# Closing a program on GpSimd's wait for the stored result, without the second barrier and without the release of the other engines

## Chip, cores, metric

One core of one Trainium2 chip in each run. The metric is the device time of one execution in microseconds (us), median of several runs; single times to 0.01 us.

## The reference

Decode step of one token, in bfloat16. The sum of three terms is written out as 1024 numbers (2 KB):

```
x   = A_x                                   # 1 x 1 x 1024
xn  = layernorm(x)
out = x + attention(xn, k_cache, v_cache, wq, wo)    # 32 query heads, 4 kv heads, 65536 keys of 128
        + mixer_mlp(xn, w1, w2, w3, w4)
```

The caches and the weights make 169.87 MB of loads, the output 2 KB of store.

## The kernel before: the parts that matter

The body streams weights and caches through three slots of SBUF. Its last act is a cast of the accumulated row and a store from ScalarE's queue:

```
    compute_w4(early, FC)

    out_t = ogpool.tile([64, 512], BF16, name="out_t", tag="og")
    nc.scalar.copy(out=out_t[:], in_=psB[0:64, :])
    nc.scalar.dma_start(out=out[0, 0, :].rearrange("(j n) -> j n", j=2),
                        in_=out_t[:].rearrange("(a b) n -> a b n", b=32)[:, 0, :])
```

Nothing in the kernel's text says how the program ends; the framework appends a closing block of 30 instructions. This is the block as it was built, with the semaphores by number: 109 counts transfers of one lane, the store's among them, 96 is the gather of the barrier, 97 its release. A gather is GpSimd's (Pool's) wait until each of the other four engines has added 1 to 96; the release is its adding of 4 to 97, of which each of the others takes 1 and goes on. The Drains between these steps do no work on data. The clear sets the program's semaphores back.

```
SP          wait 106, 105 | wait 107, 103 | wait 108, 101 | wait 109>=64, 100 | wait 110, 102 | Drain, wait 99
ACT PE DVE SP   Drain, wait 97==0, then 96 += 1        # first gather
ACT PE DVE SP   wait 97>=1, then 97 -= 1               # first release taken
Pool        Drain | wait 96>=4, then 96 -= 4 | 97 += 4 # gather, release
Pool        Drain | range clear of the semaphores
ACT PE DVE SP   Drain, wait 97==0, then 96 += 1        # second gather
ACT PE DVE SP   wait 97>=1, then 97 -= 1
Pool        Drain | wait 96>=4, then 96 -= 4 | 97 += 4
```

Of the kernel before, what the change touches and what calls it, by code (L numbers as in the profile page):

```python
# [59 lines left out]
    entry.instructions = entry.instructions[:at] + [load] + entry.instructions[at:]  # L60


@with_exitstack
def kernel(
    ctx: ExitStack,
# [13 lines left out]
    nc = tc.nc  # L79
    nc.at_finalize(keep_loaded_weights)  # L80
    nc.at_finalize(lead_with_the_first_load)
    D = A_x.shape[-1]
    S = A_x.shape[1]
    HKV = A_k_cache.shape[1]
# [3 lines left out]
    F = B_w3.shape[1]  # L88
    DC = D // P
    FC = F // P  # L90
    UKEYS = P * ROW // DH
    assert DH == P and HQ // HKV == 8 and HKV == 4 and D == 1024 and F == 3584 and S == 1
    assert SK % UKEYS == 0 and sum(W4_PIECES) == FC
# [23 lines left out]
    class Stream:  # L117
# [17 lines left out]
        def load(self, it):  # L135
# [7 lines left out]
            elif it == "w12":  # L143
                go(out=t[:, 0:DC * D], in_=B_w1.rearrange("(p c) n -> p (c n)", c=DC))
                go(out=t[:, DC * D:2 * DC * D], in_=B_w2.rearrange("(m c) n -> m (c n)", c=DC))
            elif it == "wo":
                go(out=t[:].rearrange("p (g n) -> p g n", g=HKV),
                   in_=A_wo.rearrange("(g p j) n -> p g (j n)", g=HKV, p=P))
            elif it == "w4":
                w4_v = B_w4.rearrange("(m c) n -> m c n", c=FC)  # L150
                c0 = 0
                for n in W4_PIECES:
                    go(out=t[:, c0 * D:(c0 + n) * D], in_=w4_v[:, c0:c0 + n, :].rearrange("p c n -> p (c n)"))
                    c0 += n
# [7 lines left out]

    x_row = ogpool.tile([32, D], BF16, name="x_row", tag="og")
    nc.vector.memset(x_row[:], 0.0)
# [322 lines left out]
```

## Time and profile before

| | before |
|---|---|
| time, median of the first 3 runs | 402.19 us (402.04 to 402.21) |
| recorded span, first to last instruction of the program | 400.3 us |
| load queue, share of 16 DMA engines' span | 98.6% |
| closing block after the store has landed | 0.89 us |

Four lines of the profile's page: the span, the two DMA queues (packets, MB, share of 16 engines' span), and what HBM moved; q1 carries the loads, q10 the 2 KB transfers.

```profile
span 400.3 us, 2563 instructions
...
q1 hardware_dynamic: 4560, 169.87, 98.6%
...
q10 hardware_dynamic: 6, 0.00, 0.0%
...
HBM read 169.87 MB, written 0.00 MB: 424 GB/s over the span
```

The kernel is bound by its loads for all but the last 4 us. The chain of waits that ended last, from 380 us on (start, length, what):

```profile
379.33 17.39 DMA big<-in_B_w_dram
396.73 0.04 issue
396.77 0.40 PE psB L191 x2
397.17 0.02 issue
397.19 0.58 ACT out_t L455
```

And the last two instructions that do work, from the timeline (start, length, engine, line, operation):

```profile
397.19 0.58 ACT L455 CAST out_t<-psB 64x512 bf16<-64x512 f32 x1 [29.56 <-PE psB L191]
397.80 0.59 ACTq L456 DMA_DIRECT2D out_dram<-out_t  x1
```

The last load lands at 396.73, the cast starts at 397.19, the store is issued at 397.80. What SyncE's queue waited for from 380 us on (total us, times, longest):

```profile
SPq L482 <- DMA big<-in_B_w_dram: 17.0, 3, 15.8
SPq L482 <- DMA out_dram<-out_t: 2.7, 1, 2.7
SPq L482 <- PEq L482: 0.6, 2, 0.4
```

The second line is the end of the program: SyncE waits for the store. What comes behind it is not busy work, so no group of the page shows it. The trace holds the records all the same. The closing block, read from its instruction and semaphore records (start in us, length, engine):

```
399.439         last increment of 109: the store has landed
399.455 0.028   SP    wait 109            399.938 0.096  Pool  range clear
399.517 0.028   SP    wait 110, 102       400.063 0.034  Pool  Drain
399.582 0.007   SP    Drain, wait 99      400.142 0.017  Pool  gather
399.640 0.007   SP    Drain, 96 += 1      400.220 0.017  Pool  release, ends 400.237
399.672 0.017   Pool  gather              400.262 0.017  SP    release taken
399.751 0.017   Pool  release             400.274 0.051  PE    release taken, ends 400.325
399.832 0.078   Pool  Drain
```

Behind the program the same trace shows updates of semaphore 2, nine at a time, around the resets of all semaphores:

```
first nine updates of 2:   400.588 400.622 400.799 400.843 400.867 400.965 401.003 401.037 401.084
resets                     400.980 to 401.646
second nine updates of 2:  401.870 401.904 401.942 401.987 402.010 402.107 402.146 402.180 402.227
```

The Trainium skill, "Runtime: NRT & Kernel Launch", section "The ~15µs preamble/postamble breakdown", names them: a barrier over the five engines, a reset of the semaphores, another barrier. No record shows where the clock starts or stops.

### The profile page before, as it was taken

The page shows a single profiled execution, that of the slowest core. Times are in us where ns is not written, and L with a number is a line of the kernel's source. Part 1 is how long each engine was busy: PE and PEld are TensorE (multiplying, and loading weights), DVE is VectorE, ACT ScalarE, POOL GpSimd, SP SyncE. Part 2 cuts the span into 40 slices and gives each one's busy share as a digit, 9 for nine tenths or more (in the row PEclk, how much of TensorE's full clock was granted, in tenths as well). Part 3 has the DMA queues.
Part 4 walks back from the last instruction along what each step waited for, and adds up shares of the span by engine and source line. Part 5 has one row for each costly group of instructions (what it writes and reads, how often), then busy time and mean ns, then how long its engine had stood idle before and what let it go on. Part 6 is the DMA issues. An engine that isn't in the chain of part 4 may idle for free.

```text
span 400.3 us, 2563 instructions
## 1 busy us (share of the span) xinstructions
PE 236.0 (59%) x1348; PEld 45.2 (11%) x854; DVE 208.9 (52%) x154; ACT 27.3 (7%) x35; POOL 5.3 (1%) x28
## 2 busy tenths in 40 slices
PE   0561960591678247922965195629453946594986
PEld 0210000010200110011102010201020102000222
DVE  1601010965196549644953994279349931975040
ACT  1001010003000200020002000100100020002000
POOL 2000000000000000000000000000000000000000
PEclk9995795597669666978796789568865986697989
DMA  9998999999999999999999999999999998999895
GB/s 419 419 453 371 435 471 458 426 419 419 421 426 465 452 426 414 426 426 432 445 460 426 419 426 419 447 439 452 426 421 426 432 445 385 432 481 426 385 417 201
DMA packets 4575, 170.01 MB, mean 425 GB/s; under 512 B 467, under 2 KB 469, under 8 KB 982
## 3 DMA queue, kind: packets, MB, share of 16 engines
q1 hardware_dynamic: 4560, 169.87, 98.6%
q8 instruction: 8, 0.13, 0.1%
q14 instruction: 1, 0.01, 0.0%
q10 hardware_dynamic: 6, 0.00, 0.0%
HBM read 169.87 MB, written 0.00 MB: 424 GB/s over the span
## 4 chain that ended last, share of the span: by engine, by line
DMA 51%; DVE 26%; PE 16%; ACT 3%; another core or an unknown queue 2%; issue 1%; DVEq 0%; ACTq 0%
DMA big<-in_A_k_cache_dram 31%; DVE big L327 19%; DMA big<-in_A_v_cache_dram 10%; PE sc L332 8%; PE oacc L382 6%; DMA big<-in_A_wq_dram 6%; DMA big<-in_B_w_dram 4%; DVE p_sb L353 3%; DVE mx L337 3%; ACT p_sb L350 3%; PE psq L257 2%; DVE m L341 0%; PE pm_mx L339 0%; PE pm_mx L346 0%
## 5 line engine op out<-in xcount | busy, mean ns | idle before, releaser
L332 PE MATMUL sc<-big,qdiag 128*128 128x512 bf16 x512 | 129.5, 414 | 62.7 <-DVE big L327 57.2
L327 DVE STREAM_TRANSPOSE big<-big 128x4096 f32<-128x4096 f32 x32 | 139.4, 4413 | 49.4 <-DMA big<-in_A_k_cache_dram 49.4
L382 PE MATMUL oacc<-big,p_sb 128*32 128x512 bf16 x512 | 46.9, 539 | 34.5 <-DVE p_sb L353 34.5
L337 DVE TENSOR_REDUCE mx<-sc 128x1 f32<-128x2048 f32 x8 | 18.3, 2291 | 30.0 <-PE sc L332 30.0
L332 PEld LDWEIGHTS <-qdiag 128*128 128x128 bf16 x128 | 13.2, 103 | 174.7 <-issue 145.9
L350 ACT ACTIVATE p_sb<-sc,nball 128x2048 bf16<-128x2048 f32 x8 | 15.7, 1967 | 217.8 <-DVE nball L348 217.8
L353 DVE STREAM_TRANSPOSE p_sb<-p_sb 128x2048 bf16<-128x2048 bf16 x8 | 18.5, 2311 | 18.0 <-ACT p_sb L350 18.0
L382 PEld LDWEIGHTS <-p_sb 128*32 128x32 bf16 x512 | 17.1, 129 | 61.0 <-DVE p_sb L353 35.1
L257 PE MATMUL psh<-big,ln_rep_b 128*32 128x512 bf16 (+1 forms) x64 | 12.4, 941 | 7.6 <-DMA big<-in_B_w_dram 7.6
L421 PE MATMUL o_acc<-big,oT 128*1 128x512 bf16 x48 | 12.8, 437 | 2.4 <-ACT p_sb L350 2.4
L339 PE MATMUL pm_mx<-ident_f,mx 128*1 128x128 f32 x8 | 2.2, 273 | 19.1 <-DVE mx L337 19.1
L296 DVE STREAM_TRANSPOSE h_row<-h_row 128x896 bf16<-128x896 bf16 x1 | 1.1, 1111 | 20.8 <-ACT h_row L295 20.8
L391 DVE SCALAR_TENSOR_TENSOR og<-oacc,wb,og 128x512 f32<-128x512 f32 x4 | 3.0, 746 | 16.7 <-PE oacc L382 16.7
L191 PE MATMUL psB<-big,hT 128*1 128x512 bf16 x56 | 8.1, 424 | 0.6 <-DMA big<-in_B_w_dram 0.5
L427 DVE COPY o_rows<-o_acc 1x1024 f32<-1x1024 f32 x1 | 1.2, 1211 | 13.6 <-PE oacc L382 13.6
L205 PE MATMUL pm_ln<-ln_rowsum_a,ones_f 128*128 128x1 f32 x2 | 0.6, 348 | 12.5 <-DVE ln_rowsum_a L203 12.5
L403 PE MATMUL pm_e<-ol,sel8big 128*128 128x129 f32 x8 | 2.8, 446 | 7.9 <-DVE ol L402 7.9
L257 PE MATMUL psq<-big,ln_rep_a 128*32 128x512 bf16 x64 | 6.2, 573 | 1.5 <-DMA big<-in_A_wq_dram 1.5
L281 POOL COPY qdiag<-qx 32x32 bf16<-32x32 bf16 x16 | 3.2, 203 | 279.5 <-PE sc L332 249.6
L196 DVE STREAM_TRANSPOSE x_t<-x_row 32x256 bf16<-32x256 bf16 x4 | 2.5, 616 | 8.1 <-DMA x_row<-in_A_x_dram 8.0
L269 DVE CAST q_row<-psq 128x512 bf16<-128x512 f32 x1 | 0.7, 691 | 8.4 <-PE psq L257 8.4
L346 PE MATMUL pm_mx<-ident_f,rep 1*128 1x1 f32 x8 | 1.8, 223 | 5.0 <-DVE rep L343 5.0
(95 smaller groups left out, 73.2 us busy)
## 6 DMA issues: line engine op xcount, KB each, us to landing
big<-in_A_wo_dram SPq DMA_DIRECT2D x1, 8192.0 KB, 36.0
big<-in_B_w_dram SPq DMA_DIRECT2D x1, 7168.0 KB, 38.3
big<-in_B_w_dram SPq DMA_DIRECT2D x2, 2048.0 KB, 46.3
big<-in_B_w_dram SPq DMA_DIRECT2D x2, 1536.0 KB, 27.3
big<-in_B_w_dram SPq DMA_DIRECT2D x1, 1280.0 KB, 24.1
big<-in_B_w_dram SPq DMA_DIRECT2D x1, 1024.0 KB
big<-in_B_w_dram SPq DMA_DIRECT2D x1, 768.0 KB, 30.7
big<-in_B_w_dram SPq DMA_DIRECT2D x1, 512.0 KB, 31.5
```

Of the source, the lines that this page charges most:

```text
L191: nc.tensor.matmul(psB[32 * j:32 * j + lhsT.shape[1], :], lhsT=lhsT, rhs=rhs, start=start, stop=False, tile_position=(0, 32 * j), skip_gro ...
L257: nc.tensor.matmul(acc[32 * q:32 * q + 32, i, 0:n], lhsT=rep[:, c, :], rhs=cols(c, i, q), start=(c == 0), stop=(c == DC - 1), tile_positio ...
L281: nc.gpsimd.tensor_copy(out=qdiag[at, LEAD:].rearrange("p (x c) -> p x c", x=4)[:, :, 32 * a:32 * a + 8], in_=qx[at, :, 8 * g:8 * g + 8])
L327: nc.vector.transpose(out=words, in_=words)
L332: nc.tensor.matmul(sc[:, e, :], lhsT=qdiag[:, c0:c0 + P], rhs=cols[:, s, e, :, b2, :, r], start=(s == 0 and b2 == 0 and r == 0), stop=(s = ...
L337: nc.vector.reduce_max(out=mx[:], in_=sc[:].rearrange("p e n -> p (e n)"), axis=AX.X)
L350: nc.scalar.activation(out=p_sb[:], in_=sc[:], func=ACTF.Exp, bias=nball[:, b:b + 1], scale=SCALE, accum_out=group["lall"][:, b:b + 1])
L353: nc.vector.transpose(out=flat, in_=flat)
L382: nc.tensor.matmul(oacc[32 * q:32 * (q + 1), :], lhsT=pT[:, e, 32 * t:32 * (t + 1)], rhs=vt[:, :, e, t, :], start=(e == 0 and t < 4), stop ...
L391: nc.vector.scalar_tensor_tensor(out=og[:], in0=oacc[:], scalar=wb[:, 1:2], in1=og[:], op0=ALU.mult, op1=ALU.add)
L403: nc.tensor.matmul(pe[:, 0:DH + 1], lhsT=sel8big[:], rhs=ol[:], start=True, stop=True)
L421: nc.tensor.matmul(tail["rows"][0:1, h2, :], lhsT=oT[g][:, j:j + 1], rhs=wt[:, g, j, 512 * h2:512 * (h2 + 1)], start=(g == 0 and j == 0), ...
```

## The change

Intent: the program ends sooner after its result is stored. SyncE no longer waits for the store, so the gather can be passed while the store flies; GpSimd waits for it just ahead of the clear; nobody is released, and nothing follows the clear. The diff, cut to its core:

```
+def close_on_the_store(nc):
+    ...
+    clear = max(n for n, i in enumerate(kept) if i.opcode == "ISA" and i.engine == mybir.EngineType.Pool)
+    kept = kept[:clear + 1]
+    ...
+    for i in kept:
+        if i is end or i.name == end.name:
+            i = mybir.InstDrain(... on_wait=[w for w in waits if w.id not in stored], on_update=[]))
+        elif i.opcode == "EventSemaphore" and i.engine != mybir.EngineType.Pool:
+            continue
+        elif i.opcode == "EventSemaphore" and not i.sync_info.on_wait:
+            landed = mybir.InstEventSemaphore(... on_wait=final, on_update=[]))
+            continue
+        elif i.opcode == "ISA":
+            new.append(landed)
+        new.append(i)
+    last.instructions = new
...
+    nc.at_finalize(close_on_the_store)
```

More of the change, by code (lines that the diff above doesn't have):

```diff
@@ L60, in lead_with_the_first_load @@
     entry.instructions = entry.instructions[:at] + [load] + entry.instructions[at:]
+def close_on_the_store(nc):
+    blocks = [block for function in nc.m.functions for block in function.blocks]
+    last = next(b for b in reversed(blocks) if any(i.opcode == "Drain" for i in b.instructions))
+    store = next(i for b in reversed(blocks) for i in reversed(b.instructions) if i.opcode == "DMACopy")
+    stored = {u.id for u in store.sync_info.on_update}
+    kept = list(last.instructions)
+    clear = max(n for n, i in enumerate(kept) if i.opcode == "ISA" and i.engine == mybir.EngineType.Pool)
+    kept = kept[:clear + 1]
+    end = next(i for i in kept if i.engine == mybir.EngineType.SP and i.opcode == "Drain")
+    waits = list(end.sync_info.on_wait)
+    final = [w for w in waits if w.id in stored]
+    assert len(final) == 1 and not end.sync_info.on_update
+    new = []
+    for i in kept:
+        if i is end or i.name == end.name:
+            i = mybir.InstDrain(name=i.name, engine=i.engine, debug=i.debug, ins=[], outs=[], sync_info=mybir.SyncInfo(
+                on_wait=[w for w in waits if w.id not in stored], on_update=[]))
+        elif i.opcode == "EventSemaphore" and i.engine != mybir.EngineType.Pool:
+            continue
+        elif i.opcode == "EventSemaphore" and not i.sync_info.on_wait:
+            landed = mybir.InstEventSemaphore(name=i.name, engine=i.engine, debug=i.debug, ins=[], outs=[],
+                                              sync_info=mybir.SyncInfo(on_wait=final, on_update=[]))
+            continue
[3 more added lines that the diff above has]
+    last.instructions = new
 @with_exitstack
```

## The prediction

> **What bounds the kernel now.** The transfers. The page's queue table gives the load queue 98.6% of 16 DMA engines' span, at 424 GB/s. The chain of waits ends with: last piece of w4 lands at 396.73 us, two matmuls 0.40, cast of the output 0.58 (397.19), store issued on ScalarE at 397.80. The trace's semaphore records show the store's last increment at 399.44, 1.64 us after the issue began. The recorded span ends at 400.33. So the closing block costs 0.89 us after the output has landed, and only this and what follows it are touched; the other 399 us stay.
>
> **The closing block before (instruction records that the views do not count as busy).** SyncE sees the store at 399.455, needs two more waits and two drains (end 399.65); GpSimd's gather starts 399.672, its release 399.751, its drain 399.832, the range clear of the semaphores 399.938 (0.096 long), a drain 400.063, the second gather 400.142, the second release 400.220. The other engines take the second release at 400.26 to 400.27; TensorE's record ends 400.325.
>
> **What changes.** SyncE no longer waits for the store, so the only gather completes when ScalarE's drain behind the store issue ends (398.92 before, 0.5 us before the store lands). GpSimd's gather and drain are then hidden in the store's flight, finished near 399.1. GpSimd waits for the store itself. Added: one wait of about 0.02 us, seen about 0.02 us after 399.44. Then the next GpSimd instruction starts about 0.08 us after it (the spacing of neighbouring ones before, 0.079 and 0.081): clear at about 399.54, done at 399.64. Removed from the chain: SyncE's leg and the first gather, release and drain between landing and clear (0.40 us of 0.50 in all), and everything after the clear (0.29 us). Nothing else moves: no transfer, no buffer.
>
> **On the critical path.** All of it, as nothing ends later than this chain: the recorded span should fall 0.69 us, to 399.64.
>
> What the timed figure makes of it depends on what follows. The Trainium skill, "Runtime: NRT & Kernel Launch", section "The ~15µs preamble/postamble breakdown", lists a barrier of all engines and a reset of semaphores after the kernel. The trace agrees: updates of semaphore 2 run from 400.59 to 401.08, the resets from 400.98 to 401.65, a second barrier to 402.23. In the first barrier the third update comes 0.177 us after the second, in the second barrier 0.038: the third engine arrived late, and I take it for GpSimd, the last to be done with two releases. Then its finish is what the barrier waits for and the gain passes on nearly whole: clear 0.40 earlier plus 0.24 of issue slots behind it, about 0.65 us. If another engine was the late one, the gain may reach 0.8 us; if a hidden cost in GpSimd's exit follows the clear, 0.5.
>
> **Prediction.** 402.19 - 0.65 = 401.54 us, range 401.0 to 402.0. That is 0.16%, far below 2%: faster by over 2% 0.5%, within 2% 99%, slower 0.5%.
>
> **What would show it.** Span 399.5 to 399.8; last record the range clear on GpSimd; SyncE's wait for the store (2.7 us in its queue's waits) gone; gather passed at about 398.95; clear about 0.1 us after the store's last increment; store's flight still 1.6 us; first updates of semaphore 2 from the other engines already near 399.2, the third near 400.15.
>
> **What would make it wrong.** A chip-to-chip or run-to-run shift of the 399 us of streaming larger than 0.65 us (the three runs before lie within 0.17 us); a store that flies longer[...]; an end of the timed window that lies before the barrier, or is set by another engine.

## The result, and the profile after

| | before | after |
|---|---|---|
| time, median of 6 runs each | 402.19 us (402.01 to 402.38) | 401.74 us (401.56 to 401.81) |
| ratio, 95% interval | | 0.9989 (0.9976 to 1.0001) |

The time lies in the predicted range, 0.2 us above the predicted value; the gain is 0.45 us by the medians where 0.65 was forecast.

The page's lines after:

```profile
span 399.7 us, 2547 instructions
...
q1 hardware_dynamic: 4560, 169.87, 98.7%
...
q10 hardware_dynamic: 6, 0.00, 0.0%
...
HBM read 169.87 MB, written 0.00 MB: 425 GB/s over the span
```

The chain of waits after, from 380 us on:

```profile
379.51 17.39 DMA big<-in_B_w_dram
396.90 0.04 issue
396.94 0.40 PE psB L221 x2
397.34 0.02 issue
397.36 0.58 ACT out_t L485
```

The end of the timeline, and then the waits of SyncE's queue:

```profile
397.36 0.58 ACT L485 CAST out_t<-psB 64x512 bf16<-64x512 f32 x1 [29.43 <-PE psB L221]
397.97 0.59 ACTq L486 DMA_DIRECT2D out_dram<-out_t  x1
```

```profile
SPq L512 <- DMA big<-in_B_w_dram: 16.9, 4, 14.5
SPq L512 <- ACT out_t L485: 1.0, 1, 1.0
```

Two things are to be seen. SyncE's wait of 2.7 us for the store is gone. And the whole tail begins 0.17 us later than before (396.90 against 396.73): that is the streaming, which the change does not touch, and it hides part of the gain in this pair of traces. The closing block after, from the records:

```
399.128 0.017  Pool  gather          399.617        last increment of 109: the store has landed
399.209 0.077  Pool  Drain           399.641 0.096  Pool  range clear, wait 109; ends 399.737
first nine updates of 2:   397.618 399.250 400.264 400.308 400.331 400.429 400.467 400.501 400.548
resets                     400.447 to 401.111
second nine updates of 2:  401.335 401.370 401.408 401.451 401.475 401.572 401.610 401.645 401.691
```

To take the streaming out, count from the store's landing, in the profiled run of each kernel. The last row uses the clock's time of that same run, as if it began with the first instruction. Nothing recorded ahead of the program contradicts this: the last nine updates of semaphore 2 before the first instruction keep their places to 0.005 us in all fourteen traces.

| us from the landing to | before | after | difference |
|---|---|---|---|
| start of the clear | 0.50 | 0.02 | -0.48 |
| end of the span | 0.89 | 0.12 | -0.77 |
| third update of the barrier behind the program | 1.36 | 0.65 | -0.71 |
| last update of the second barrier | 2.79 | 2.07 | -0.71 |
| end of the timed run (time minus landing) | 2.67 | 2.19 | -0.48 |

The first four rows carry the gain through, as predicted. The last row does not: the timed figure ends 0.117 us short of the last update before, and 0.119 us past it after. So 0.24 us of what the program saved is given back where no record shows it.

### The profile page after: what moved, and what is told of

Its sections match the earlier page's. It is cut to its first block, busy times and chain, and to the rows that moved or that the text cites. A ratio compares the mean times of both kernels' runs of the same rounds, so it can differ in the third digit from the quotient of the medians.

```text
span 399.7 us, 2547 instructions
## 1 busy us (share of the span) xinstructions
PE 229.8 (57%) x1348; PEld 44.8 (11%) x854; DVE 209.0 (52%) x154; ACT 27.3 (7%) x35; POOL 5.4 (1%) x28
## 4 chain that ended last, share of the span: by engine, by line
DMA 52%; DVE 26%; PE 16%; ACT 3%; another core or an unknown queue 2%; issue 1%; DVEq 0%; ACTq 0%
DMA big<-in_A_k_cache_dram 31%; DVE big L357 19%; DMA big<-in_A_v_cache_dram 10%; PE sc L362 8%; PE oacc L412 6%; DMA big<-in_A_wq_dram 5%; DMA big<-in_B_w_dram 4%; DVE p_sb L383 3%; DVE mx L367 3%; ACT p_sb L380 3%; PE psq L287 1%; PE pm_mx L369 0%; DVE m L371 0%; PE pm_mx L376 0%
## 5 line engine op out<-in xcount | busy, mean ns | idle before, releaser
L412 PE MATMUL oacc<-big,p_sb 128*32 128x512 bf16 x512 | 43.0, 509 | 34.5 <-DVE p_sb L383 34.5
L451 PE MATMUL o_acc<-big,oT 128*1 128x512 bf16 x48 | 12.0, 415 | 2.4 <-ACT p_sb L380 2.4
```

Of the source, the lines that this page charges most:

```text
L412: nc.tensor.matmul(oacc[32 * q:32 * (q + 1), :], lhsT=pT[:, e, 32 * t:32 * (t + 1)], rhs=vt[:, :, e, t, :], start=(e == 0 and t < 4), stop ...
L451: nc.tensor.matmul(tail["rows"][0:1, h2, :], lhsT=oT[g][:, j:j + 1], rhs=wt[:, g, j, 512 * h2:512 * (h2 + 1)], start=(g == 0 and j == 0), ...
```

## The experiments

Three theories of the missing quarter of a microsecond: H, chance of the streaming; S, a slower stream in the changed program; G, something given back behind the records. All programs gave correct results. In the list of each result, "landing" is the store's last increment, "last" the last update of the second barrier, "offset" the time of the profiled run minus "last" counted from the first instruction.

### The two kernels once more

Edit: a comment. Five runs each, on one chip, together with the next two.

> The kernel before, unchanged but for a comment, to see how large a difference of two equal programs is. Every theory: 402.2 us and a ratio of 1.000, within 0.0004; trace as before: store landed near 399.4, 0.89 us from the landing to the end of the span, 2.79 us from the landing to the last update of the second barrier after the program. If it differs by 0.2 us or more from its twin, the shortfall of the change (0.45 us of the 0.71 that its trace shows) is chance.

> The changed kernel, unchanged but for a comment. In the trace of the first run the stretch from the store's landing to the last update of the second barrier fell by 0.71 us (2.79 to 2.07), the median time by 0.45. Theory H (all handed on, the rest is chance of the streaming): the time falls by 0.6 to 0.8 us. Theory S (the streaming of the changed program is slower by about 0.18 us): the fall is 0.45 again, and the store lands near 399.6 again. Theory G (part of the gain is given back outside of these records): the fall is 0.45 again, with the store landing at 399.4 to 399.6 by chance, and time minus last update is again about 0.24 us larger than for the kernel before.

Measured: the twin of before 402.13 us, ratio 1.0000 (0.9987 to 1.0012), landing to last 2.79, offset -0.119. The twin of after 401.53 us against 402.16, ratio 0.9984 (0.9972 to 0.9997), landing at 399.40, landing to last 2.10, offset +0.116.

What follows: S falls, since the changed program's stream landed 0.22 us earlier this time than in its first profile. The timed gain was 0.63 us here and 0.45 before: the streaming moves medians of five or six by that much. The offset does not move: it comes back to 0.003 us. So H explains the spread of the medians, G holds for the step itself, and it is read from single profiles better than from medians. The sets of several executions agree, those without a kept trace included: time minus span is 1.78 to 1.80 us on average for the kernel before and its twin (23 executions) and 2.08 us for the changed kernel (11). The traces give 1.78, and 2.07 and 2.10.

### One part alone: only the wait is moved

```
-        SP waits for 109 ahead of its drain
+        Pool: range clear waits for 109       # release, second gather, second release stay
```

> One part of the change alone: GpSimd, not SyncE, waits for the store, just ahead of the clear; first release, second barrier and second release stay. Theory that GpSimd's arrival is what counts: the clear starts 0.02 to 0.03 us after the landing instead of 0.50, all after it stays, so landing to end of span is 0.41 us and the time falls by 0.47 us (402.19 to 401.7). Rival, that the barrier after the program is held by another engine (then the second barrier in the program costs what the change gained): less than 0.2 us.

Measured: 401.64 us against 402.16, ratio 0.9987 (0.9975 to 1.0000). Clear 0.02 us after the landing, end of span 0.41, third update 0.89, last 2.31, offset -0.118. Time minus landing 2.195 us.

What follows: the sum holds to 0.01 us (2.671 - 2.195 = 0.476), and the offset is that of before. Counted from the landing to the end of the timed run, this part alone is as good as the whole change (2.193 and 2.215 us in the two profiles of the changed kernel).

### The other part alone: nothing behind the clear

```
-        second gather and second release on all engines
         # first release stays, SP still waits for the store ahead of the first gather
```

> The other part alone: everything after the clear is gone (second gather, second release), SyncE still waits for the store ahead of the first gather and the first release stays. Theory that GpSimd's arrival counts: landing to clear stays 0.50 us, the third update of the runtime's first barrier comes 0.24 us earlier after the landing (1.36 to 1.12), and the time falls by 0.24 us. Rival (the other engines count): they leave after the first release at 399.80 instead of 400.27, so the time falls by 0.45 us.

SyncE's waits from 380 us on show that the wait for the store stayed as before:

```profile
SPq L491 <- DMA big<-in_B_w_dram: 17.0, 3, 15.8
SPq L491 <- DMA out_dram<-out_t: 2.7, 1, 2.7
SPq L491 <- PEq L491: 0.2, 1, 0.2
```

Measured: 402.17 us against 402.16, ratio 1.0000 (0.9986 to 1.0014). Landing to clear 0.50 us, third update 1.12, last 2.55: all as expected, 0.24 us sooner than before. But the offset is +0.247, and time minus landing 2.80 us against 2.67.

What follows: taking the second barrier away brings the third update and all later ones 0.24 us closer to the landing and gains nothing in the time. The forecast of 0.24 us for the time missed as well, and only its part about the records held. The rival, that the other engines' departure counts, forecast 0.45 us and falls. The offset is now at its third value, about -0.12, +0.12, +0.25, in programs in which the engines other than GpSimd have, against before, the same number of instructions, three fewer, two fewer. (Time minus span says the same of all five executions: 2.21 us on average here, 1.81 in gate_only.)

### The length of the engines' programs

```
+    pads: InstDrain without waits; Pool 4 ahead of its gather; ACT, PE, DVE, SP 3 each behind their last drain
```

The pads are hidden: GpSimd is idle there, and the other engines are done before the store lands.

> The changed kernel with as many instructions on every engine as the kernel before: four empty drains on GpSimd ahead of its gather (it is idle there), three on each other engine behind its own drain, all hidden in the store's flight; the order of arrival stays as in the changed kernel. What is to be explained: time minus last update of the runtime's second barrier is -0.118 us in the kernel before, its twin and gate_only, but +0.117 in the changed kernel twice and +0.247 in no_second. Theory L (the length of the engines' programs sets what follows the last barrier): -0.118 again, time about 401.35. Theory E (the engines that leave early, without the second barrier, set it): +0.117 again, time 401.6.

> The same with the four drains on GpSimd alone. Theory L with GpSimd as the engine: time minus last update -0.118; with another engine: +0.117; theory E: +0.117. Landing to end of span 0.12 us in all of them.

> The same with the three drains on ScalarE, TensorE, VectorE and SyncE alone. Theory L with one of these as the engine: time minus last update -0.118; with GpSimd: +0.117; theory E: +0.117.

Measured: pads on all engines, five runs, 401.46 us against 402.11, ratio 0.9984 (0.9971 to 0.9996); landing to end of span 0.12, to last 2.07, offset -0.117. Pads on GpSimd alone, one run: offset +0.114. Pads on the other four, one run: offset -0.113.

What follows: theory L (the length of the engines' programs sets the offset) holds and E (engines that leave early set it) falls. Instructions that do nothing, on engines that have nothing left to do, take about 0.24 us from the time: minus landing, 1.955 us with them and 2.193 or 2.215 without. The median itself missed the expected 401.35 us by 0.11, with a landing at 399.585. The engine is not GpSimd.

### Which engine

```
+    three drains on PE and three on ACT          /    three on PE and three on DVE
```

> The changed kernel with three empty drains on TensorE and three on ScalarE only. One of four engines is taken to be the one whose program length sets the piece behind the last barrier. Time minus last update of the second barrier -0.115 us: it is TensorE or ScalarE; +0.115: it is VectorE or SyncE. If it is a size between, more than one engine takes part.

> The changed kernel with three empty drains on TensorE and three on VectorE only. Time minus last update -0.115 us: it is TensorE or VectorE; +0.115: ScalarE or SyncE. Together with the run beside it one engine is named: both low TensorE, only the other low ScalarE, only this low VectorE, neither SyncE.

Measured: with TensorE and ScalarE 401.38 us, offset -0.116; with TensorE and VectorE 401.87 us, offset +0.118. (The second also landed 0.26 us later: streaming.)

What follows: it is ScalarE, if one engine alone sets the offset; the next run, with a pad on ScalarE alone, moves it.

### How the size depends on ScalarE's length

```
 changed kernel:  + one drain on ACT behind its last drain
 kernel before:   + one drain on ACT ahead of its first gather drain
```

> The changed kernel with one empty drain more on ScalarE, so two shorter than before, as in no_second. If the length of ScalarE's program alone sets the piece: time minus last update +0.247, as in no_second; landing to last update 2.07. If no_second's larger piece came of its release or its SyncE wait: not +0.247 (then +0.116, or -0.118).

> The kernel before with one empty drain more on ScalarE, ahead of its first gather drain, where ScalarE has 0.5 us to spare; nothing else is changed. ScalarE's program is then one longer. So far: length of before, or 4 shorter, time minus last update -0.118; 3 shorter +0.116; 2 shorter +0.247. If the piece comes back every four instructions (one longer is like three shorter): +0.116, time 0.23 us up. If only shorter programs pay: -0.118. The landing to last update stretch stays 2.79 us in both.

Measured: the changed kernel with one drain more, offset +0.254, landing to last 2.08: length alone makes no_second's larger piece. The kernel before with one more: offset -0.120, so the "every four" guess fell. But this program was also slower, 2.758 us from landing to the end of the timed run against 2.671. In its second barrier the second update comes 0.123 us after the first (401.964, 402.087) where all other programs show 0.034 or 0.035. The second update is ScalarE's (below), so ScalarE came 0.09 us late to that barrier.

What follows: ScalarE's length moves the timed end. One longer than before, 0.09 us shows ahead of the second barrier; two and three shorter, 0.37 and 0.24 us more than at the length of before show in the offset. The traces narrow the first: the resets of semaphores 54 to 104, which follow the eighth update of the first barrier by 0.10 us and so are taken for ScalarE's, run through in at most 0.27 us in every trace, this one too, so the 0.09 us was lost behind them. That the other two pieces are also ScalarE's lost time, behind the second barrier, is argued and not shown. One guess is a stall at a fixed place of ScalarE's instruction stream that slides past the barrier, such as the refill that the Trainium skill describes in "Runtime: NRT & Kernel Launch", section "Instruction fetch mechanics" (the engines read their instructions in blocks, and a block's edge costs something that is "mostly hidden"). No record shows a fetch there: in all fourteen traces the last packet of the two instruction queues (q8 and q14) starts near 383 us. And a sliding stall does not by itself say why nothing shows at the length of before and at four shorter. So the stall stays a guess; that the offset hangs on ScalarE's length is shown.

### A shorter close

```
 closing block:   SP: all other waits, Drain wait 99, then wait 109
-                 every gather, release and clear
```

The runtime resets the semaphores itself behind its first barrier (the resets above), so the program's own clear is left to it.

> No gather and no clear in the program at all: each engine ends its program when its work is done, SyncE alone waits for the store (the reset of all semaphores that follows the program clears what is left). If the runtime's first barrier waits for the engine that comes last and GpSimd was that one only for its wait and clear, SyncE now holds it: landing to end of span 0.03 us, landing to the last update of the second barrier 1.75 to 1.95 us instead of 2.07 to 2.10. Time 401.3 to 401.6; theory L leaves the offset behind the last update open (other lengths again), theory E says +0.117 or more.

SyncE's waits from 380 us on; here it is SyncE that holds on for the store, and no barrier of the program shows:

```profile
SPq L499 <- DMA big<-in_B_w_dram: 16.9, 4, 14.5
SPq L499 <- DMA out_dram<-out_t: 1.6, 1, 1.6
SPq L499 <- ACT out_t L472: 1.0, 1, 1.0
```

Measured: 400.79 us (400.63 to 400.91) against 402.11, ratio 0.9967 (0.9953 to 0.9981), correct. Landing to end of span 0.03 us, to last 1.48, offset -0.117, time minus landing 1.36 us.

What follows: the expectation was too timid: from landing to last it took 1.48 us where 1.75 to 1.95 was expected, and the time came 0.5 us below its range of 401.3 to 401.6. It had no figure for what GpSimd's exit costs. The updates of the runtime's first barrier, with the last record of the engine that each belongs to:

```
kernel        engine     its last record ends   its update    between
after         GpSimd     399.737                3rd, 400.264  0.527
before        GpSimd     400.237                3rd, 400.799  0.562
after         ScalarE    399.095                2nd, 399.250  0.155
no_clear_SP   SyncE      399.585                5th, 399.688  0.103
no_clear_SP   GpSimd     285.431                3rd, 399.151  0.039 after the 2nd: not late
```

Which engine an update belongs to is inferred from what moves it: the third follows GpSimd's end by 0.53 to 0.56 us in every program where GpSimd clears after the store has landed, and comes at once where it has been idle since 285 us; the second moves with ScalarE's pads. Here GpSimd was a costly engine to end on and SyncE a cheap one. No run has GpSimd hold the wait without the clear, so the exit of the engine and an after-effect of the clear are not told apart. ScalarE's program is four shorter than before here, and the offset is the low one, which was luck. One caution: this close relies on the reset behind the program, seen in these traces, and only five executions of it are on record, one of them profiled.

## Why the prediction was right, and where it was not

| step of the prediction | forecast | measured |
|---|---|---|
| nothing but the closing block moves | stream unchanged | shown: the landing varies by chance, 399.34 to 399.68 in programs with the same body |
| gather hidden in the store's flight | passed near 398.95 | 399.13, with the whole tail 0.17 later |
| store's flight, issue to last increment | 1.6 us | 1.65 us |
| landing to clear | 0.10 us | 0.024 us: the wait rides on the clear |
| landing to end of span | 0.20 us | 0.12 us |
| third update after the landing | 0.71 us | 0.65 us |
| first updates of the others | near 399.2 | 397.62 and 399.25: TensorE went much earlier |
| records' gain handed on | "the gain passes on nearly whole" | 0.71 us in the records, 0.46 to 0.48 in the timed run |

The time was right, and so was the chain of the records: the barrier behind the program waits for GpSimd, and its wait for the store is what counts. The term that was mis-sized is the gain's way to the timed figure. The prediction had 0.65 us; the records gave 0.71, of which 0.476 comes from moving the wait (gate_only) and 0.24 from dropping everything behind the clear. Those 0.24 us are real in the records (no_second, and 1.955 against 2.195 us once ScalarE's length is restored), and 0.24 us are given back, in the offset, because ScalarE's program became three instructions shorter. The prediction had named "set by another engine" as a way to be wrong, but it had no number for it and did not think of length. That 0.65 us comes so near the 0.63 us of the second set is luck: the records gave 0.06 us more than forecast, 0.24 us was given back, and the streaming's chance made up the rest. The range of 401.0 to 402.0 us was no test of the mechanism either; gate_only (401.64) and pad_all (401.46) lie in it too.

The streaming's chance is as large as these terms: medians of two equal five- or six-run sets of the changed kernel differ by 0.2 us. The timed verdict of the change is "same" at the 2% step, with an interval of its ratio that includes 1 in the first set and ends at 0.9997 in the second. The decomposition rests on the profiled runs counted from the landing, where equal programs agree to 0.03 us, and on time minus span in all executions.

Left open: what ScalarE does in those tenths, why nothing shows at the length of before and at four shorter, and what starts and ends the timed window.

## What to carry to other kernels

Count the end of a program from the landing of its last store to the end of the timed run, not to the last recorded instruction: the runtime's barriers lie in between, and in these traces only the engine that came last to the first of them held it up. Let an engine with a cheap exit (here SyncE, 0.10 us against GpSimd's 0.53) hold the last wait, hide every other wait in the store's flight, and after any change of the instruction count, even on an idle engine, check time minus last record before crediting or blaming the edit. All this, the shorter close included, was worth 1.3 us of 402, so it matters only where the stream itself has nothing left to give.

## What the Trainium skill lacked or had wrong

- "Runtime: NRT & Kernel Launch", section "The ~15µs preamble/postamble breakdown": it gives about 1.5 us each for the barrier and the reset behind a kernel. Here, before the change, the first barrier took 0.50 us from its first to its last update (0.76 from the program's last record), the resets 0.67 us and the second barrier 0.36 us. Its figure of about 355 ns for the run through the five engines agrees with the second barrier's 357 ns, but the steps are not equal: 0.02 to 0.10 us.
- The same section has no cost of an engine's exit: where the engine itself was waited for, GpSimd's update comes 0.53 to 0.56 us after its last record's end, ScalarE's 0.11 to 0.16 (with its drain in the program), SyncE's 0.10.
- No page has it that the number of ScalarE's instructions moves the timed end: -0.12 us against the last update at the length of before, +0.12 with three fewer, +0.25 with two fewer, -0.12 with four fewer. "Instruction fetch mechanics" on that page calls a block's edge "mostly hidden"; if this is one, it was not.
- "DMA: Bandwidth & Descriptors", section "Anatomy of one DMA — SWDGE (gpsimd) path", gives a fixed cost of about 2.0 us for a transfer on GpSimd's path; it has no such fit for a store from ScalarE's queue. The 2 KB store from there took 1.63 to 1.65 us from the start of its issue to its last increment, in all fourteen traces.
